# Third token tile of the second layer by products of half tiles, with weight buffers and weight steps moved

## The chip, the core and the metric

The kernel runs on one core of a Trainium2 chip. The core's engines work from queues of their own, each in the order in which its instructions were issued: TensorE (PE; its weight loads are listed apart as PEld), VectorE (DVE), ScalarE (ACT), GpSimd (POOL), and SyncE (SP), which issues most of the DMAs. The metric is the device time of one execution in microseconds (us), the median of the runs.

## The reference

```
# attention: b=2, h=8, s=768, d=64; blocks of 64, a decaying state per head
x = attention(q, k, v, lam)            # reshaped to 1536 tokens x 512
h = x @ w_in                           # 512 -> 2048
g = where(h >= 1, h, where(h <= -1, 0, (h + 1)**2 / 4))
x = g @ w_out                          # 2048 -> 512
y = (sigmoid(x @ w_gate) * (x @ w_val)) @ w_out2   # 512 -> 1536 -> 512
```

Tokens and results are float32, the weight matrices are float64. Every product of the two layers is made from high and low parts: high times high, low times high, high times low, three matmuls each.

## The kernel before

Attention runs first (lines 671 to 1001), in 16 units of 384 tokens. `u_load` fetches a unit's q, k, k and v rows as four slices; `scores` needs the first two. Attention's outputs are written as the high and low parts `xh` and `xl`. Beside it the first weight pieces are converted and the first layer begins.

A weight matrix is fetched in 68 pieces of 128 x 512 (`pieces`, line 73). Pieces 0 to 31 belong to the first layer; the second layer has 36, six for each group of two units: gate and value of both units, then both output slices. Group 18 has pieces 38 to 43, group 20 has 44 to 49, group 22 has 50 to 55, group 24 has 56 to 61, group 26 has 62 to 67. One step of the pipeline is a round (`w_steps`, line 175). In round k `w_float(k-1)` joins two limbs on VectorE (L122, L126), `w_high(k-2)` rounds to the high part on ScalarE (L130), `w_words(k)` takes the words of a raw tile apart on ScalarE (L108 into `r`, L115 and L116 into `c`), and `w_low(k-2)` makes the remainder on VectorE (L134). Buffers are rings: ten finished tiles (`NWP`), three raw tiles (`NRAW`), two `c` tiles and five `r` tiles. A round is put off while the finished tile whose buffer it needs is not in `used`.

Tokens are three tiles of 512. For tiles 0 and 1 together a pair of gate and value weights is multiplied by seven block products in place of eight (`pair`, line 430). It needs sums and differences of the weight blocks (`w_forms`, four half-width operations, L152) and their high and low parts (`w_forms_split`, line 155: ScalarE's copy L159, a subtraction L160). In the second layer's pairs both are on POOL (`prog["forms"] = pool`, line 625). Splits wait until `prog["room"]` allows them.

The order is written out by hand. In `second_layer` group 16 takes all three tiles one by one; from line 626 groups n0 = 18, 20, 22, 24, 26 follow with units n0 and n1 = n0 + 1: pair of n0, the projections of the group before for tile 2, pair of n1, projections of tiles 0 and 1, and between them tile 2 of each unit on its own (`single`, two calls of `hidden` with 12 matmuls each). A product is six matmuls: p0, p1, p0 (L449 copies it), p2, p0 (the fifth, after which L454 copies), p0, p2. A product that goes on accumulating in p0 waits until ScalarE has copied it. `pair_act` makes the high part, remainder, sigmoid and multiply of a result. `flush` adds four finished projections to `part` on VectorE (L306). Four PSUM banks serve the products, four the projections.

Of the kernel before, what the change touches and what calls it, by code (L numbers as in the profile page):

```python
# [7 lines left out]
F32 = mybir.dt.float32  # L8
F32R = mybir.dt.float32r
# [3 lines left out]
ALU = mybir.AluOpType  # L13
# [16 lines left out]
CST = 4 + PADW + P  # L30
NS = 2 * CU - 1
FORE, AFT = (6, 7), (5, 6)
JOBS = {4: ("W0", "", "", "F0", "", ""), 5: ("H0 W1", "", "F1", "", "H1 W2", ""),
# [5 lines left out]
WARM = 8  # L39
NWP, NRAW = 10, 3  # L40


@with_exitstack
def fused_kernel(ctx: ExitStack, tc: tile.TileContext, qkv, qd, cst, w1, w2, out):
# [42 lines left out]

    prog = {"loaded": 0, "round": 0, "room": True, "forms": dve, "split": False}
    used = set()

    attention_over = []

    def w_load():
        i = prog["loaded"]
        if i >= len(pieces) or i >= NRAW + max(0, prog["round"] - 1):
            return
        prog["loaded"] += 1
        n, o = pieces[i]
        raws[i] = rawp.tile([P, 512], I64, tag="raw", name=f"raw{i}")
        src = w1[n] if n < NF1 else w2[n - NF1]  # L100
        sp.dma_start(out=raws[i], in_=src[:, o:o + 512])

    def w_words(i):
        word = raws[i].bitcast(U32).rearrange("p (n two) -> p n two", two=2)
        lo, hi = word[:, :, 0], word[:, :, 1]
        r = tp.tile([P, 512], F32, tag="r", bufs=5, name=f"wr{i}")
        c = tp.tile([P, 512], I32, tag="c", name=f"wc{i}")
        act.activation(r, hi.bitcast(F32), AF.Copy, scale=2.0 ** -112)  # L108
        if not attention_over:
            act.activation(c, lo, AF.Copy, scale=2.0 ** -29)  # L110
            tmps[i] = r, c, hi
            return

        limb = lambda dt: c.bitcast(dt).rearrange("p (n two) -> p n two", two=2)
        act.activation(limb(U16)[:, :, 0], lo, AF.Copy, scale=2.0 ** -29)  # L115
        act.activation(limb(F16)[:, :, 1], hi.bitcast(F32), AF.Copy, scale=2.0 ** -60)  # L116
        tmps[i] = r, c, None
# [10 lines left out]
    def w_high(i):  # L128
        ws[i] = wp.tile([P, 2, 512], F32R, tag="w", name=f"w{i}")
        act.activation(ws[i][:, 0], tmps[i][0], AF.Copy)  # L130
# [24 lines left out]
    def w_forms_split(n):  # L155
        tiles = []
        for i, f in enumerate(forms[n]):
            t = fp.tile([P, 2, 512], F32R, tag="s", name=f"s{n}_{i}")
            act.activation(t[:, 0], f, AF.Copy)  # L159
            prog["forms"].tensor_tensor(out=t[:, 1], in0=f, in1=t[:, 0].bitcast(F32),  # L160
                                        op=ALU.subtract)
            tiles.append(t)
# [4 lines left out]
    def w_round():  # L167
        split = [n for n in forms if n not in ready and prog["split"]]
        if split and not prog["room"]:
            return  # L170
        w_steps()
        for n in split:
            w_forms_split(n)

    def w_steps():
        k = prog["round"]
        if k - 2 >= len(pieces):
            return
        if k - 2 >= NWP and k - 2 - NWP not in used:
            return  # L180
        prog["round"] += 1
        if 0 <= k - 1 < len(pieces):
            w_float(k - 1, dve)
        making = 0 <= k - 2 and k - 2 not in ws
        if making:
            w_high(k - 2)
        if k < len(pieces):
            while prog["loaded"] <= k:
                w_load()
            w_words(k)  # L190
        if making:
            w_low(k - 2, dve)
            w_forms(k - 2)
        w_load()
# [74 lines left out]
    def project(n, t, gs, first, last, now=True):  # L269
# [7 lines left out]
        for j in range(4):  # L277
            js = slice(j * P, (j + 1) * P)
            if two:
                ops = [(gh[:, js], w[:, 0]), (gh[:, js], w[:, 1]), (gl[:, js], w[:, 0])]  # L280
            else:
# [126 lines left out]
    def forms_second():  # L408
# [6 lines left out]
        return [x1, y2, x2, y1]  # L415

    def product(o, w, c, x, start):

# [11 lines left out]
    def pair(n):  # L430
# [29 lines left out]
        product(p2, s24, hw, x_at(1, 1), False)  # L460
        dve.tensor_tensor(out=r[1], in0=r[1], in1=p2, op=ALU.add)
        yield r

# [135 lines left out]
    def second_layer(waiting):  # L599
# [26 lines left out]
        for n0 in range(NF1 + GF, NF1 + NF2, GF):  # L626
# [8 lines left out]
            w_round()  # L635
            for _ in range(2 if n0 == NF1 + GF else 4):
                next(a)
            prog["room"] = False
            for p in waiting:
                w_round()  # L640
                project(*p, now=False)
            flush(p[0], p[1], (0, 1))
            ra, ga = next(a), {}
            flush(p[0], p[1], (2, 3))
            prog["room"] = True
            xa = pair_act(n0, ra, ga)
            for _ in range(5):
                next(b)
                next(xa)
            w_round()  # L650
            project(n0, 0, ga[0], True, False)
            w_round()
            rb, gb = next(b), {}
            ha = single(n0, 2, pair_act(n1, rb, gb))
            w_round()
# [15 lines left out]
    with ExitStack() as actx:  # L671
        kp = actx.enter_context(tc.tile_pool(name="kp", bufs=1))
        up = actx.enter_context(tc.tile_pool(name="up", bufs=UB))
# [10 lines left out]
        def u_load(i, js=range(2)):  # L684
# [10 lines left out]
            if i < NEARLY:  # L695

                t = [wp.tile([P, 2, 512], F32, tag="w", name=f"u{i}_{j}")
                     .rearrange("p a b -> p (a b)")[:, 0:2 * UT]
                     .rearrange("p (a t) -> p a t", a=2) for j in js]
                for j in js:  # L700
# [175 lines left out]
        def values(i):  # L876
# [11 lines left out]
            if i >= NEARLY:  # L888
                u_load(i + UB)

# [117 lines left out]
    for c in "hl":  # L1008
        xt[c] = late.tile([P, 3, HK, TT], F32R, name=f"xt{c}")
    attention_over.append(1)  # L1010
    with tc.manual_schedule():
        psx.close()
        for c in "ah":
            banks[c] = ctx.enter_context(
# [73 lines left out]
```

## Time and profile before

| | us |
|---|---|
| median of 3 runs (586.93 to 587.21) | 587.18 |
| the profiled execution's own time | 587.08 |
| its span, first to last instruction | 585.2 |
| TensorE busy | 579.0 |
| VectorE busy | 441.1 |
| ScalarE busy | 370.8 |

The span is the time between the first and the last instruction; 1.9 us of the execution lie around it. Busy time is the union of an engine's records. A matmul's record is longer than the step from one matmul to the next, so the starts tell the pace. In a timeline a row gives the start and the length in us, and behind it, in brackets, how long the engine had been idle and what ended that. Groups of the second layer begin at 344.56 (18), 390.80 (20), 437.04 (22), 483.28 (24) and 529.52 us (26).

### The profile page before, as it was taken

How to read it: one execution, taken by the hardware profiler on the slowest of the kernel's cores; microseconds unless marked ns; L12 is line 12 of the kernel's file. 1: busy time of each engine (PE TensorE's matmuls, PEld its weight loads, DVE VectorE, ACT ScalarE, POOL GpSimd, SP SyncE). 2: the span in 40 equal slices, each digit the busy share in tenths (PEclk: the TensorE clock that was granted, in tenths of full speed). 3: DMA queues.
4: the chain of work that ended last, by engine and by line, in shares of the span. 5: the costliest groups of instructions: out<-in, count | busy, mean ns of one | idle time of the engine just before them, and what ended most of it. 6: DMA issues, size and time to landing. Idle time of an engine off the chain costs nothing.

```text
span 585.2 us, 8061 instructions
## 1 busy us (share of the span) xinstructions
PE 579.0 (99%) x3074; PEld 481.4 (82%) x3074; DVE 441.1 (75%) x722; ACT 370.8 (63%) x653; POOL 71.3 (12%) x72
## 2 busy tenths in 40 slices
PE   8999999999999999999999999999999999999997
PEld 8987788888888888888888888888888888888885
DVE  5988798888897979797888996793693694684444
ACT  4678775996777777777874976772672773541220
POOL 3540000000000000000000002421412332150000
PEclk9999999999999999999999999999999999999999
DMA  8983340122112222221312223231231140000013
GB/s 336 401 317 109 108 144 1 37 92 80 46 72 73 72 73 72 73 72 38 107 38 72 84 96 109 72 109 36 73 108 37 38 120 22 1 0 2 0 73 143
DMA packets 15734, 52.00 MB, mean 89 GB/s; under 512 B 1744, under 2 KB 1872, under 8 KB 15696
## 3 DMA queue, kind: packets, MB, share of 16 engines
q1 hardware_dynamic: 15552, 51.39, 26.4%
q8 instruction: 24, 0.39, 0.3%
q10 hardware_dynamic: 144, 0.10, 0.1%
q14 instruction: 14, 0.11, 0.1%
HBM read 48.33 MB, written 3.15 MB: 88 GB/s over the span
## 4 chain that ended last, share of the span: by engine, by line
PE 93%; DMA 2%; DVE 2%; ACT 2%; issue 1%; SPq 0%; POOL 0%; DVEq 0%; POOLq 0%; ACTq 0%
PE a L284 38%; PE p L423 26%; PE h L229 8%; PE h L231 8%; PE h L230 8%; DMA u<-in_qkv 2%; PE s L821 2%; PE x L882 1%; PE x L901 1%; PE uu L839 1%; DVE part L306 0%; DVE r L265 0%; ACT r L256 0%; ACT r L261 0%; ACT gh L248 0%
## 5 line engine op out<-in xcount | busy, mean ns | idle before, releaser
L284 PE MATMUL a<-gh,w 128*128 128x512 f32 x384 | 118.6, 390 | 0.5 <-DVE w L134 0.5
L306 DVE TENSOR_TENSOR part<-part,a 128x512 f32<-128x512 f32 x132 | 83.3, 682 | 12.1 <-PE a L284 11.9
L284 PE MATMUL a<-w,gh 128*128 128x512 f32 x288 | 88.7, 389 | 0.0
L229 PE MATMUL h<-xh,w 128*128 128x512 f32 x224 | 87.6, 391 | 0.0
L230 PE MATMUL h<-xh,w 128*128 128x512 f32 x224 | 87.2, 389 | 0.0
L231 PE MATMUL h<-xl,w 128*128 128x512 f32 x224 | 87.1, 389 | 0.0
L284 PEld LDWEIGHTS a<-gh,w 128*128 128x128 f32 x384 | 72.0, 188 | 15.9 <-DVE w L134 0.9
L284 PE MATMUL a<-gl,w 128*128 128x512 f32 x192 | 74.7, 389 | 0.0
L284 PEld LDWEIGHTS a<-w,gh 128*128 128x128 f32 x288 | 54.1, 188 | 11.3
L284 PE MATMUL a<-w,gl 128*128 128x512 f32 x144 | 56.0, 389 | 0.0
L152 POOL TENSOR_TENSOR wr<-wr 128x256 f32<-128x256 f32 x16 | 13.1, 821 | 340.6 <-DVE w L134 340.0
L130 ACT ACTIVATE w<-wr 128x512 fp32r<-128x512 f32 x68 | 42.3, 622 | 17.7 <-DVE wr L126 17.5
L134 DVE TENSOR_TENSOR w<-wr,w 128x512 fp32r<-128x512 f32 x65 | 48.4, 745 | 4.0 <-ACT w L130 3.8
L126 DVE CUSTOM_DVE_ANT_0 wr<-wr,wc 128x1024 uint16<-128x1024 uint16 x68 | 48.1, 708 | 3.4 <-ACT wc L116 0.2
L229 PEld LDWEIGHTS h<-xh,w 128*128 128x128 f32 x224 | 42.1, 188 | 9.1 <-ACT r L261 0.2
L231 PEld LDWEIGHTS h<-xl,w 128*128 128x128 f32 x224 | 42.1, 188 | 8.8
L230 PEld LDWEIGHTS h<-xh,w 128*128 128x128 f32 x224 | 42.1, 188 | 8.6
L115 ACT ACTIVATE wc<-raw 128x512 uint16<-128x512 uint32 x61 | 47.9, 785 | 0.0
L108 ACT ACTIVATE wr<-raw 128x512 f32<-128x512 f32 x68 | 45.0, 662 | 4.2 <-POOL s L160 3.6
L116 ACT ACTIVATE wc<-raw 128x512 f16<-128x512 f32 x61 | 47.0, 771 | 0.0
L248 ACT ACTIVATE gh<-r 128x512 fp32r<-128x512 f32 x40 | 24.9, 624 | 31.7 <-DVE r L265 21.8
L284 PEld LDWEIGHTS a<-gl,w 128*128 128x128 f32 x192 | 36.0, 188 | 7.5
(121 smaller groups left out, 1028.7 us busy)
## 6 DMA issues: line engine op xcount, KB each, us to landing
raw<-in_w SPq DMA_DIRECT2D x68, 512.0 KB, 3.5
u<-in_qkv SPq DMA_DIRECT2D x22, 384.0 KB, 8.1
u<-in_qkv SPq DMA_DIRECT2D x4, 768.0 KB, 7.9
out<-part SPq DMA_DIRECT2D x12, 256.0 KB, 2.1
part<-in_qkv SPq DMA_DIRECT2D x2, 384.0 KB, 8.4
cs<-in_cst ACTq DMA_DIRECT2D x1, 98.0 KB, 3.8
```

The costliest lines, as they stand in the source:

```text
L108: act.activation(r, hi.bitcast(F32), AF.Copy, scale=2.0 ** -112)
L115: act.activation(limb(U16)[:, :, 0], lo, AF.Copy, scale=2.0 ** -29)
L116: act.activation(limb(F16)[:, :, 1], hi.bitcast(F32), AF.Copy, scale=2.0 ** -60)
L126: eng.tensor_tensor(out=ri, in0=ri, in1=c, op=ALU.add)
L130: act.activation(ws[i][:, 0], tmps[i][0], AF.Copy)
L134: eng.tensor_tensor(out=ws[i][:, 1], in0=r, in1=ws[i][:, 0].bitcast(F32), op=ALU.subtract)
L229: pe.matmul(h, lhsT=wh, rhs=xh[:, k, tt], start=(k == 0), stop=False)
L230: pe.matmul(h, lhsT=wl, rhs=xh[:, k, tt], start=False, stop=False)
L231: pe.matmul(h, lhsT=wh, rhs=xl[:, k, tt], start=False, stop=(k == NP - 1))
L284: pe.matmul(accs[j], lhsT=a, rhs=b_, start=(first and m == 0), stop=(last and m == 2))
L306: dve.tensor_tensor(out=o, in0=o, in1=accs[j], op=ALU.add)
L423: pe.matmul(o, lhsT=a, rhs=b_, start=(start and k == 0 and m == 0), stop=(k == HK - 1 and m == 2), skip_group_check=True)
```

## The change

In groups 20 to 26 tile 2 is no longer made by `single` but by `pair_third`: the seven block products on two halves of the tile, 256 tokens each, for both units side by side in one bank. That is 14 times six matmuls of 256 columns for 48 of 512. The sums and differences of the token blocks are made once, in group 20 (`forms_third`, 20 forming operations, 8 high parts and 8 remainders of 256 columns), spread over the steps of the two pairs by `along`. Room for them is made by closing a pool: finished weights keep nine tiles (`NWP`) and one of the pool `extra` (pieces 9, 19, 29, 39), raw tiles two and one of the pool up to piece 48, and `c` one and one of the pool up to piece 48. Forms are split at other places of a group, and from group 20 on the subtraction is VectorE's. In rounds 8 and 9 the high part and remainder of a piece come ahead of the float of the next (`LOW_FIRST`). Piece 8 is loaded once attention is over. Unit 13 of attention is loaded in two parts.

```diff
+LOW_FIRST = (8, 9)
...
-NWP, NRAW = 10, 3
+NWP, NRAW = 9, 2
+EXTRA_W, EXTRA_RAW = (9, 19, 29, 39), 48
...
         i = prog["loaded"]
-        if i >= len(pieces) or i >= NRAW + max(0, prog["round"] - 1):
+        more = 1 if i <= EXTRA_RAW else 0
+        if i >= len(pieces) or i >= NRAW + more + max(0, prog["round"] - 1):
+            return
+        if i == 8 and not attention_over:
             return
         prog["loaded"] += 1
         n, o = pieces[i]
-        raws[i] = rawp.tile([P, 512], I64, tag="raw", name=f"raw{i}")
+        pool_ = extra["pool"] if i % 3 == 2 and i <= EXTRA_RAW else rawp
+        raws[i] = pool_.tile([P, 512], I64, tag="raw", name=f"raw{i}")
...
-        c = tp.tile([P, 512], I32, tag="c", name=f"wc{i}")
+        pool_ = extra["pool"] if i % 2 and i <= EXTRA_RAW else tp
+        c = pool_.tile([P, 512], I32, tag="c", bufs=1, name=f"wc{i}")
...
     def w_high(i):
-        ws[i] = wp.tile([P, 2, 512], F32R, tag="w", name=f"w{i}")
+        if i not in EXTRA_W:
+            ring.append(i)
+        ws[i] = (extra["pool"] if i in EXTRA_W else wp).tile([P, 2, 512], F32R, tag="w", name=f"w{i}")
         act.activation(ws[i][:, 0], tmps[i][0], AF.Copy)
...
-            prog["forms"].tensor_tensor(out=t[:, 1], in0=f, in1=t[:, 0].bitcast(F32),
-                                        op=ALU.subtract)
+            eng = dve if prog["thirds"] else prog["forms"]
+            eng.tensor_tensor(out=t[:, 1], in0=f, in1=t[:, 0].bitcast(F32), op=ALU.subtract)
...
     def w_round():
         split = [n for n in forms if n not in ready and prog["split"]]
         if split and not prog["room"]:
-            return
+            if not prog["thirds"]:
+                return
+            split = []
+        if prog["thirds"]:
+            for n in split:
+                w_forms_split(n)
         w_steps()
         for n in split:
-            w_forms_split(n)
+            if n not in ready:
+                w_forms_split(n)
...
     def w_steps():
         k = prog["round"]
         if k - 2 >= len(pieces):
             return
-        if k - 2 >= NWP and k - 2 - NWP not in used:
+        i = k - 2
+        if i in EXTRA_W[1:]:
+            if EXTRA_W[EXTRA_W.index(i) - 1] not in used:
+                return
+        elif i not in EXTRA_W and i >= NWP and i not in ws and ring[-NWP] not in used:
             return
         prog["round"] += 1
+        making = 0 <= k - 2 and k - 2 not in ws
+        low = lambda: (w_low(k - 2, dve), w_forms(k - 2))
+        if making and k in LOW_FIRST:
+            w_high(k - 2)
+            low()
         if 0 <= k - 1 < len(pieces):
             w_float(k - 1, dve)
-        making = 0 <= k - 2 and k - 2 not in ws
-        if making:
+        if making and k not in LOW_FIRST:
             w_high(k - 2)
         if k < len(pieces):
             while prog["loaded"] <= k:
                 w_load()
             w_words(k)
-        if making:
-            w_low(k - 2, dve)
-            w_forms(k - 2)
+        if making and k not in LOW_FIRST:
+            low()
         w_load()
...
             if two:
-                ops = [(gh[:, js], w[:, 0]), (gh[:, js], w[:, 1]), (gl[:, js], w[:, 0])]
+                ah, al = (g[j] if isinstance(g, list) else g[:, js] for g in (gh, gl))
+                ops = [(ah, w[:, 0]), (ah, w[:, 1]), (al, w[:, 0])]
...
+    HT = TT // 2
+    xt2 = {}
+    third = lambda x, k, b: x[:, k * HK:(k + 1) * HK, 2 * TT + b * HT:2 * TT + (b + 1) * HT]
+    def forms_third():
+        last.close()
+        pool_ = ctx.enter_context(tc.tile_pool(name="third", bufs=1, reuse_waits="tile"))
+        for c in "hl":
+            xt2[c] = pool_.tile([P, 3, HK, HT], F32R, name=f"xt2{c}")
+        f = pool_.tile([P, HT], F32, name="f3")
...
+        def form(k, i, *terms):
...
+            def forming():
+                for m, (x, y, op) in enumerate(terms):
+                    a, b = (f if z is None else at(*z).bitcast(F32) for z in (x, y))
+                    dve.tensor_tensor(out=f, in0=a, in1=b, op=op)
+            def high_():
+                act.activation(hi_at, f, AF.Copy)
+            def rests():
+                dve.tensor_tensor(out=lo_at, in0=f, in1=hi_at.bitcast(F32), op=ALU.subtract)
+            return forming, high_, rests
...
+        add, sub = ALU.add, ALU.subtract
+        for k in range(HK):
+            made = [
+                form(k, 0, ((xh, 0, 1), (xh, 0, 0), sub), (None, (xl, 0, 0), sub),
+                     (None, (xl, 0, 1), add)),
+                form(k, 1, ((xh, 1, 1), None, sub), (None, (xl, 1, 1), add)),
+                form(k, 2, ((xh, 1, 0), None, sub), (None, (xl, 1, 0), add)),
+                form(k, 3, ((xh, 1, 1), (xh, 0, 1), sub), (None, (xl, 0, 1), sub),
+                     (None, (xl, 1, 1), add)),
+            ]
+            rests = None
+            for forming, high_, after in made:
+                steps_.append((lambda a=rests, b=forming: (a and a(), b()), high_))
+                rests = after
+            steps_.append((rests, lambda: None))
+        return steps_
...
+    def pair_third(n0):
...
+        ns = (n0, n0 + 1)
+        hw = HK * P
+        raw = lambda k, b: (third(xh, k, b), third(xl, k, b))
+        t_at = lambda i: (xt2["h"][:, i], xt2["l"][:, i])
+        p0, p1, p2 = (bank(f"t{n0}_{i}") for i in range(3))
+        r = [rest(f"v{n0}_{i}") for i in range(3)]
+        g, v = ([ws[index[n, o]] for n in ns] for o in (0, 512))
+        s31, s24 = ([ready[n][i] for n in ns] for i in range(2))
...
+        def both(o, w, c, x, start):
+            for i in range(2):
+                product(o[:, i * HT:(i + 1) * HT], w[i], c, x, start and i == 0)
+        both(p0, g, 0, raw(0, 0), True)
+        act.activation(r[0], p0, AF.Copy)
+        yield
+        both(p1, g, hw, raw(1, 0), True)
+        dve.tensor_tensor(out=r[0], in0=r[0], in1=p1, op=ALU.add)
+        yield
+        both(p0, s24, 0, t_at(1), False)
+        act.activation(r[1], p0, AF.Copy)
+        yield
+        both(p2, s31, hw, t_at(0), True)
+        yield
+        both(p0, s31, 0, raw(0, 1), False)
+        act.activation(r[2], p0, AF.Copy)
+        dve.tensor_tensor(out=r[2], in0=r[2], in1=p2, op=ALU.add)
+        act.activation(r[0], r[0], AF.Sigmoid)
+        yield
+        both(p0, v, hw, t_at(2), False)
+        dve.tensor_tensor(out=r[0], in0=r[0], in1=p0, op=ALU.mult)
+        both(p2, s24, hw, raw(1, 1), False)
+        dve.tensor_tensor(out=r[1], in0=r[1], in1=p2, op=ALU.add)
+        used.update(index[n, o] for n in ns for o in (0, 512))
         yield r
...
-            for _ in range(2 if n0 == NF1 + GF else 4):
-                next(a)
-            prog["room"] = False
+            thirds = n0 > NF1 + GF
+            if n0 == NF1 + 2 * GF:
+                made = forms_third()
+            def along(step):
+                begin, end = made.pop(0) if thirds and made else (None, None)
+                if begin:
+                    begin()
+                x = step()
+                if end:
+                    end()
+                return x
+            for _ in range(4 if thirds else 2):
+                along(lambda: next(a))
+            prog["room"], prog["thirds"] = thirds, thirds
             for p in waiting:
                 w_round()
                 project(*p, now=False)
+                prog["room"] = False
             flush(p[0], p[1], (0, 1))
             ra, ga = next(a), {}
             flush(p[0], p[1], (2, 3))
-            prog["room"] = True
+            prog["room"] = not thirds
...
             for _ in range(5):
-                next(b)
+                along(lambda: next(b))
                 next(xa)
             w_round()
             project(n0, 0, ga[0], True, False)
+            along(lambda: None)
...
             w_round()
...
-            ha = single(n0, 2, pair_act(n1, rb, gb))
+            xb = pair_act(n1, rb, gb)
+            if thirds:
+                c = pair_third(n0)
+                for _ in range(5):
+                    next(c)
+                    next(xb)
+                project(n1, 0, gb[0], False, True)
+                rc, gc = next(c), {}
+                xc = pair_act(n0, rc, gc)
+                next(xc)
+                prog["room"] = True
+                w_round()
+                prog["room"] = False
+                next(xc)
+                next(xc)
+                project(n0, 1, ga[1], True, False)
+                next(xc)
+                next(xc)
+                project(n1, 1, gb[1], False, True)
+                waiting = []
+                for i, n in enumerate((n0, n1)):
+                    at = lambda x: [gc[j // 2][x][:, i * HT + j % 2 * P:i * HT + j % 2 * P + P]
+                                    for j in range(4)]
+                    waiting.append((n, 2, (at(0), at(1)), n == n0, n == n1))
+                continue
+            ha = single(n0, 2, xb)
...
                 t = [wp.tile([P, 2, 512], F32, tag="w", name=f"u{i}_{j}")
                      .rearrange("p a b -> p (a b)")[:, 0:2 * UT]
-                     .rearrange("p (a t) -> p a t", a=2) for j in js]
+                     .rearrange("p (a t) -> p a t", a=2) if 2 * i + j < NWP else
+                     kp.tile([P, 2, UT], F32, name=f"u{i}_{j}") for j in js]
...
             if i >= NEARLY:
-                u_load(i + UB)
+                for js in ((0,), (1,)) if i + UB == NHALVES + 1 else ((0, 1),):
+                    u_load(i + UB, js)
...
+    last = ctx.enter_context(ExitStack())
+    extra["pool"] = last.enter_context(tc.tile_pool(name="extra", bufs=1, reuse_waits="tile"))
     attention_over.append(1)
     with tc.manual_schedule():
         psx.close()
+        w_load()
```

## Rows read from the trace of the kernel before

**Rows 1.** Busy us (share of the span) and instructions of each engine, whole span.

```profile
PE 579.0 (99%) x3074; PEld 481.4 (82%) x3074; DVE 441.1 (75%) x722; ACT 370.8 (63%) x653; POOL 71.3 (12%) x72
```

**Rows 2.** Busy us (and instructions) of each engine by stretch, groups 20 and 22.

```profile
core 0: us, PE busy (x) PEld busy (x) DVE busy (x) ACT busy (x) POOL busy (x), PEclk, DMA share, GB/s
...
390.80:437.00 46.20, 46.20 (x205) 38.30 (x204) 31.13 (x49) 26.27 (x46) 12.64 (x12) 1.00 0.23 69
437.00:483.30 46.30, 46.30 (x206) 38.32 (x206) 31.23 (x49) 26.29 (x46) 12.63 (x12) 1.00 0.23 69
```

**Rows 3.** Timeline, TensorE and its loads, 500 to 503: start, us, engine, line.

```profile
500.05 0.39 PE L423 MATMUL p<-xl,w 128*128 128x512 f32 x1
500.05 0.41 PEld L423 LDWEIGHTS p<-xh,w 128*128 128x128 f32 x2
...
502.77 0.39 PE L423 MATMUL p<-xtl,s 128*128 128x512 f32 x1
```

**Rows 4.** Groups by line and shape, weight loads: xcount, busy us, mean ns, idle before.

```profile
L423 PEld LDWEIGHTS p<-xh,w 128*128 128x128 f32 x128 | 24.0, 188 | 5.0
...
L882 PEld LDWEIGHTS x<-pT,u 128*64 128x64 f32 x180 | 9.6, 137 | 1.2 <-issue 0.7
```

**Rows 5.** Timeline, weight loads in attention, 24 to 29.

```profile
23.97 1.42 PEld L821 LDWEIGHTS s<-u 64*128 64x128 f32 x24 [0.17 <-issue]
...
27.44 0.72 PEld L839 LDWEIGHTS uu<-u,kd 128*64 128x64 f32 x20
```

**Rows 6.** Timelines, VectorE and TensorE, 70 to 74.

```profile
70.85 0.42 DVE L122 TENSOR_SCALAR wr<-wr 128x512 uint32<-128x512 uint32 x1
...
71.91 0.68 DVE L134 TENSOR_TENSOR w<-wr,w 128x512 fp32r<-128x512 f32 x1
...
71.75 0.39 PE L284 MATMUL a<-gh,w 128*128 128x512 f32 x1
72.65 0.50 PE L284 MATMUL a<-gh,w 128*128 128x512 f32 x1 [0.51 <-DVE w L134]
```

**Rows 7.** Timeline, TensorE, 34 to 36.

```profile
34.94 0.94 PE L821 MATMUL s<-u 64*128 64x128 f32 x12 [0.21 <-DMA u<-in_qkv]
```

**Rows 8.** Groups by line, the subtraction of a form's split on either engine.

```profile
L160 DVE TENSOR_TENSOR s<-wr,s 128x512 fp32r<-128x512 f32 x16 | 10.3, 685 | 0.0
...
L160 POOL TENSOR_TENSOR s<-wr,s 128x512 fp32r<-128x512 f32 x16 | 24.9, 1575 | 81.1 <-ACT s L159 81.1
```

**Rows 9.** Timelines, VectorE and POOL, 460 to 470, one row of each.

```profile
464.12 1.39 DVE L134 TENSOR_TENSOR w<-wr,w 128x512 fp32r<-128x512 f32 x1 [0.31 <-ACT w L130]
...
463.13 3.54 POOL L160 TENSOR_TENSOR s<-wr,s 128x512 fp32r<-128x512 f32 x2 [19.36 <-ACT s L159]
```

**Rows 10.** Timeline, VectorE, 328.9 to 331.4: two dependent operations of 256 columns.

```profile
329.66 0.89 DVE L152 TENSOR_TENSOR wr<-wr,wr 128x256 f32<-128x256 f32 x2
```

**Rows 11.** Groups by line and shape, ScalarE's copy of 256 columns.

```profile
L860 ACT ACTIVATE ld<-qp 128x256 f32<-128x256 f32 x7 | 2.8, 404 | 0.0
```

**Rows 12.** Timeline, VectorE, 436 to 441: the turn from group 20 to 22.

```profile
435.57 2.48 DVE L306 TENSOR_TENSOR part<-part,a 128x512 f32<-128x512 f32 x4
437.96 0.42 DVE L122 TENSOR_SCALAR wr<-wr 128x512 uint32<-128x512 uint32 x1
438.41 0.69 DVE L126 CUSTOM_DVE_ANT_0 wr<-wr,wc 128x1024 uint16<-128x1024 uint16 x1
439.75 0.69 DVE L134 TENSOR_TENSOR w<-wr,w 128x512 fp32r<-128x512 f32 x1 [0.64 <-ACT w L130]
```

**Rows 13.** Timeline, ScalarE, 437 to 445: the same turn.

```profile
438.60 0.60 ACT L443 ACTIVATE q<-p 128x512 f32<-128x512 f32 x1 [3.67 <-PE p L423]
...
440.17 0.80 ACT L115 ACTIVATE wc<-raw 128x512 uint16<-128x512 uint32 x1
440.82 0.78 ACT L116 ACTIVATE wc<-raw 128x512 f16<-128x512 f32 x1
441.44 0.59 ACT L449 ACTIVATE q<-p 128x512 f32<-128x512 f32 x1
```

More of the change, by code (lines that the diff above doesn't have):

```diff
@@ L84, in fused_kernel @@
     whole, forms, ready = {}, {}, {}
-    prog = {"loaded": 0, "round": 0, "room": True, "forms": dve, "split": False}
+    prog = {"loaded": 0, "round": 0, "room": True, "forms": dve, "split": False, "thirds": False}
     used = set()
     attention_over = []
+    extra = {}
+    ring = []
     def w_load():
         i = prog["loaded"]
-        if i >= len(pieces) or i >= NRAW + max(0, prog["round"] - 1):
+        more = 1 if i <= EXTRA_RAW else 0
+        if i >= len(pieces) or i >= NRAW + more + max(0, prog["round"] - 1):
+            return
+        if i == 8 and not attention_over:
             return
@@ L415, in forms_second @@
         return [x1, y2, x2, y1]
+    HT = TT // 2
[7 more added lines that the diff above has]
+        f = pool_.tile([P, HT], F32, name="f3")
+        steps_ = []
+        def form(k, i, *terms):
+            at = lambda x, j, b: third(x, j, b)[:, k]
+            hi_at, lo_at = ((at(xh, 0, 1), at(xl, 0, 1)) if i == 3 else
+                            (xt2["h"][:, i, k], xt2["l"][:, i, k]))
+            def forming():
[23 more added lines that the diff above has]
+        return steps_
     def product(o, w, c, x, start):
@@ L461, in pair @@
         dve.tensor_tensor(out=r[1], in0=r[1], in1=p2, op=ALU.add)
+        yield r
+    def pair_third(n0):
[31 more added lines that the diff above has]
+        used.update(index[n, o] for n in ns for o in (0, 512))
         yield r
@@ L651, in second_layer @@
             project(n0, 0, ga[0], True, False)
+            along(lambda: None)
+            assert not thirds or not made
             w_round()
             rb, gb = next(b), {}
-            ha = single(n0, 2, pair_act(n1, rb, gb))
+            xb = pair_act(n1, rb, gb)
[24 more added lines that the diff above has]
+            ha = single(n0, 2, xb)
             w_round()
@@ L671, in fused_kernel @@
     with ExitStack() as actx:
-        kp = actx.enter_context(tc.tile_pool(name="kp", bufs=1))
+        kp = extra["pool"] = actx.enter_context(tc.tile_pool(name="kp", bufs=1))
         up = actx.enter_context(tc.tile_pool(name="up", bufs=UB))
```

## Prediction

> **What bounds the kernel now.** I read the engine totals first: TensorE is busy 99% of the span, VectorE 75% [rows 1]. The totals average stages, so next the table by stretch: groups 20 and 22 of the second layer take 46.2 and 46.3 us, TensorE fills both, VectorE is busy 31 us in each [rows 2]. A busy TensorE need not be at its peak, so I look at starts: between 500.05 and 502.77 twelve matmuls of 512 columns begin, one per 226.7 ns [rows 3], and 204 of them (84 for two pairs, 48 for the singles, 72 projections) make 46.24 us, the whole group. Nothing waits: the group costs what its matmuls cost. Every term below is therefore matmul time saved, or a new wait of TensorE.
>
> **The third tile by block products.** In groups 20, 22, 24 and 26 the two units' singles (48 matmuls of 512 columns) give way to seven products of 6 matmuls for each of two units, 84 of 256 columns. Removed: 48 x 226.7 = 10.88 us a group. Added: 84 times a price that no row shows, since nothing here streams 256 columns. From below: at exactly half, 113.3 ns. In attention two row groups renew a 128-column weight load every (1.42-0.19)/11 = 112 ns [rows 5], so loads of that size can follow each other that fast. From above: the record of such a load is 188 ns, 50 ns more than one of 64 columns [rows 4], and 188 would be the price if a matmul had to wait for the whole record. For a value: in attention a pair of 128-column matmuls takes 112 ns and one of 64 columns (0.72-0.14)/9.5 = 61 ns [rows 5], so 51 ns are per 64 columns and some 10 ns are fixed. With 10 fixed, 256 columns cost (226.7-10)/2 + 10 = 118 ns. I take that, as the row with the same engine and element size, with 113 to 124 as its near ends. Then a group saves 10.88 - 84 x 0.118 = 0.95 us, four save **3.8 us** (1.9 to 5.4). Break-even is 10.88/84 = 129.5 ns.
>
> The Trainium skill (TensorE: Matmul & The Clock Gate, Back-to-back issue gap) gives N/2.4 + 2.5 ns warm: 109 ns at 256, which would save 1.7 us a group. The same rule gives 215.8 ns at 512, where the rows have 226.7, so the trace disagrees and I keep 118.
>
> **Two remainders first, unit 13 in parts.** TensorE stops once behind the weight pipeline: a matmul starts at 72.65 where 71.98 was due, behind the remainder (L134) that VectorE begins at 71.91, after two operations of the next piece from 70.85 [rows 6]. Put first, it begins at 70.85 and ends before the matmul is due: 0.67 us back, and the slower first starts after the stop, together **0.8 us**. It cannot cost more than the two operations it passes, 1.1 us, which work a round ahead. Unit 13: TensorE waits 0.21 us for its load [rows 7], starts included some **0.3 us** (0 to 0.4), back if queries and keys land first.
>
> **Moves that I cost at nothing.** The extra pool keeps ten weight tiles, three raw tiles and two c tiles until piece 39 or 48, each buffer reused at the old distance. Piece 8's load moves behind the end of attention on SP's queue, some 58 us, and all later loads queue behind it; ScalarE reads it at 70.57 in the trace and a load takes 3.5 us in the median, so 8 us cover it. Without that cover it would cost what it is late. Finished weights stand a group ahead of their use before; by the new ring piece 49 waits for 40, and then 53 is made at the end of group 20, needed 15 us into group 22. Cover remains.
>
> **What VectorE and ScalarE get.** A third tile by blocks needs seven operations of each for four before: +3 each. Subtractions of four forms move from POOL (1,575 ns) to VectorE (685 ns) [rows 8], +2.7 us a group. POOL's use does slow VectorE: a remainder takes 1.39 us beside one [rows 9]. In group 20 come 28 operations of 256 columns, 0.45 us each [rows 10], 12.6 us, and 8 ScalarE copies of 0.40 [rows 11], all within its first 27 us, beside three rounds of 1.7 and 17 operations of 0.60 us, 15.3 us, of VectorE's other work there. And from piece 49 on there is one c tile: ScalarE's words of a piece wait for VectorE's float of the piece before, issued in the same round. Queued behind on ScalarE are the evacuations that TensorE waits for.
>
> **Stall in group 20.** Times from the group's start. Starting as group 22 does now, VectorE ends the flushes at 0.9, float at 2.1 and the remainder at 3.4 [rows 12]; three forming operations then end at 4.7, the high part on ScalarE at 5.1, and the copy of p0, due 4.4, is done at 5.6: the fifth product, due 5.44, waits 0.2. Each form costs its operations and 0.45 for the trip to ScalarE. Carried on this way, the second pair's copy of p0 ends 0.35 late for its sixth product, and its multiply, behind float and remainder, frees a bank 0.7 late for the third tile's second product. Together **1.3 us** (0.5 to 2.5).
>
> **Stall at the start of groups 22 and 24.** After the third tile's last product (ends 40.0) VectorE queues one addition (40.2), two form subtractions, float and remainder to 43.7, and the remainder of the first half to 44.3. ScalarE's words may begin their second part only after float, at 43.2; they take 1.27, and the sigmoid behind them ends at 45.1. Then multiply (45.9), high part (46.55), remainder (47.2), the four flushes (0.60 apart) to 49.6, and the next float to 50.75. The group turned at 45.4, so this float ends 5.3 into the next one, where before it ended at 2.1 [rows 12]. There ScalarE's words wait for it (5.4), and behind their 1.27 the copy of p0 begins at 6.7, where before it began at 4.40 [rows 13], the group having begun at 437.04. It ends at 7.3; the fifth product was due at 5.44: 1.9 us. Beside POOL's forming, which starts at 43.8, multiply and remainder take up to 0.5 longer [rows 9]: 2.1 us each, **4.2 us** (2.5 to 5.5). Group 26 has no words left in that round: nothing. Add 0.2 for the bank of the third tile in 22 and 24. Before, two c tiles and a light tail (flushes over at 0.9) cover all this.
>
> **Sum**, from the profiled execution's own 587.08 us (span 585.2 plus 1.9 around it; the median of the runs is 587.18, 0.1 above): -3.8 -0.8 -0.3 +1.3 +4.2 +0.2 = +0.8, so **587.9 us**. The saving is real and is given back at three starts of groups. Its own range: most saving and least stall 587.1 - 5.4 - 1.2 + 3.0 = 583.5; least saving and most stall 587.1 - 1.9 - 0.8 + 8.2 = 592.6; I call it 585.0 to 591.0.
>
> **Rivals.**
> 1. *The tail is in time.* If VectorE and ScalarE run the chain faster than I add it up, or enough of it lies beside the last projections (10.9 us from the third tile's end to the fifth product, against my chain of 12.7), the starts of 22 and 24 cost nothing. Then 587.1 - 4.9 + 0 to 1.5 = 582.2 to 583.7, say 583. For it: TensorE has not one gap in these groups now, and VectorE is still idle a third of each group [rows 2]. Against it: the chain is serial, and the idle third lies elsewhere.
> 2. *Halves at 112 ns*, the pace at which attention renews its loads [rows 5], the stalls as worked: 84 x 0.112 = 9.41, four times 1.47 saved, 587.1 - 5.9 - 1.1 + 5.7 = 585.8. By the skill's 109 ns it would be 584.9.
> 3. *The weight load sets the pace* (slower). In the trace each load begins with the matmul before it and is recorded at 188 ns, hidden under 226.7 [rows 3, 4]. If the next matmul needs all of it, a half costs 188: 84 x 0.188 = 15.8, +4.9 a group, 587.1 + 19.6 - 1.1 + about 1 = 607. It decides from 129.5 ns on. Against it: 112 ns between loads [rows 5], there with two row groups in turn.
> 4. *Load and stream one after the other.* 100 for the load (128 columns at 50 ns per 64 [rows 4]) and 113 for the stream are 213 ns a half: 17.9 for 10.9, +7.0 a group, 587.1 + 28.0 - 1.1 = 614. Against it: 226.7 ns for 512 columns leaves no 100 for a load, unless a column takes far less than the 0.42 ns that I count. The Trainium skill (TensorE: Matmul & The Clock Gate, Packing small matmuls) says weight loads overlap running matmuls only where the row group differs; it would mean this rival, and the 226.7 of whole-array matmuls speaks against it here.
>
> **How the numbers follow.** Forecast 0.57, rival 1 0.27, rival 2 0.08, rival 3 0.05, rival 4 0.03. Some 0.2% (1.2 us) is what a measurement can tell from no change: faster is below 586.0, slower above 588.4. Of the forecast's 0.57, 0.13 lie below, 0.22 between, 0.22 above. Faster: 0.27 + 0.08 + 0.13 = 0.48, shaded to 0.46 as rival 2 reaches into the middle; same 0.23; slower 0.31. Cases of both signs share the chance, so the range runs from rival 1 without any stall (582.0) to the top of the forecast (591.0), leaving out rivals 3 and 4 and about a tenth beyond the ends.
>
> **What the profile would show.** Right: starts 118 ns apart in the new products; no gap near 72; one TensorE gap of about 2 us at the fifth product of groups 22 and 24, ended by ScalarE's copy of p0, whose words waited for VectorE's float; three small gaps in group 20; none in group 26. Groups of about 46.6 (20), 47.4 (22, 24) and 45.3 us (26). Wrong: starts above 130 ns, groups of 45.3 without gaps, or the waits on another engine than ScalarE.

## The result, and the profile after

| | before | after |
|---|---|---|
| median, us | 586.99 (6 runs) | 591.47 (6 runs) |
| ratio, 95% interval | | 1.0071 (1.0058 to 1.0084) |
| the profiled execution, us | 587.08 | 591.48 |
| its span, us | 585.2 | 589.6 |

The change made the kernel slower by 0.7%. Forecast was 587.9 us in a range of 582.0 to 591.0; the time lies above it. First the table by stretch: busy us (and instructions) of TensorE, its loads, VectorE, ScalarE and POOL. The rows are groups 20, 22 and 24, and as many us from the start of group 26 on as a group took before; the last columns are the granted clock of TensorE, the DMA share and GB/s.

```profile
core 0: us, PE busy (x) PEld busy (x) DVE busy (x) ACT busy (x) POOL busy (x), PEclk, DMA share, GB/s
390.10:436.20 46.10, 46.05 (x241) 39.08 (x240) 37.79 (x73) 25.08 (x46) 4.50 (x6) 1.00 0.14 43
436.20:484.70 48.50, 45.84 (x242) 39.32 (x241) 34.43 (x56) 28.56 (x49) 7.58 (x9) 1.00 0.22 66
484.70:534.70 50.00, 47.34 (x241) 40.37 (x240) 34.41 (x56) 28.61 (x49) 7.45 (x9) 0.97 0.18 53
534.70:580.90 46.20, 46.20 (x245) 39.92 (x244) 28.89 (x45) 14.77 (x26) 2.14 (x3) 1.00 0.09 32
```

Beside [rows 2]: group 20 takes as long as before, group 22 takes 2.2 us more and group 24 3.8 us more. TensorE is idle for 2.7 us in each of groups 22 and 24, and in group 24 its granted clock is 0.97 as well. VectorE is still idle for 14 and 16 us there. Group 26 has no gap. The timeline of TensorE shows where the idle time stands (start, us, engine, line; in brackets the idle time and what ended it), first in group 22, then in group 24.

```profile
441.44 0.39 PE L497 MATMUL p<-xtl,s 128*128 128x512 f32 x1
444.49 0.73 PE L497 MATMUL p<-xh,s 128*128 128x512 f32 x2 [2.66 <-ACT q L523]
...
489.87 0.39 PE L497 MATMUL p<-xtl,s 128*128 128x512 f32 x1
492.92 0.73 PE L497 MATMUL p<-xh,s 128*128 128x512 f32 x2 [2.66 <-ACT q L523]
...
494.36 0.63 PE L497 MATMUL p<-xl,s 128*128 128x512 f32 x1
494.79 1.05 PE L309 MATMUL a<-w,gh 128*128 128x512 f32 x2
```

Both gaps are the forecast's: the fifth product of the first pair, waiting for ScalarE's copy of p0 (L523, L449 before). From start to start they are 3.05 us where 0.23 are due, 2.82 us lost. After the second, from 494.0 on, the matmuls start 0.43 us apart instead of 0.227 for some 3.4 us. Granted clock around both, same columns with TensorE alone:

```profile
441.40:444.50 3.10, 0.44 (x3) 1.00 0.00 0
444.50:448.00 3.50, 3.50 (x15) 1.00 0.50 150
489.80:493.00 3.20, 0.54 (x4) 1.00 0.00 0
493.00:494.00 1.00, 1.00 (x5) 0.98 0.51 123
494.00:497.40 3.40, 3.40 (x10) 0.51 0.34 123
497.40:500.00 2.60, 2.60 (x13) 1.00 0.00 0
```

The clock went to its lower level of 1.2 GHz after the second gap, 1.0 us behind its end, and not after the first. That cost 1.6 us, the difference of groups 24 and 22. Five of the six executions took 591.3 to 591.9 us at a mean granted clock of 0.996 or 0.997; the sixth took 589.55 at 0.999, by its clock without the fall.

Next, VectorE and ScalarE around the turn from group 20 to 22 (at 436.22), the view of [rows 12, 13].

```profile
430.96 0.69 DVE L572 TENSOR_TENSOR v<-v,t 128x512 f32<-128x512 f32 x1 [0.64 <-PE t L497]
431.56 1.29 DVE L172 TENSOR_TENSOR s<-wr,s 128x512 fp32r<-128x512 f32 x2
...
433.22 0.69 DVE L135 CUSTOM_DVE_ANT_0 wr<-wr,wc 128x1024 uint16<-128x1024 uint16 x1
...
435.88 1.20 DVE L688 TENSOR_TENSOR v<-v,v 128x512 f32<-128x512 f32 x1 [0.76 <-ACT v L686]
437.84 1.21 DVE L681 TENSOR_TENSOR gl<-v,gh 128x512 fp32r<-128x512 f32 x1 [0.76 <-ACT gh L690]
438.97 2.47 DVE L331 TENSOR_TENSOR part<-part,a 128x512 f32<-128x512 f32 x4
441.36 0.41 DVE L131 TENSOR_SCALAR wr<-wr 128x512 uint32<-128x512 uint32 x1
441.81 0.69 DVE L135 CUSTOM_DVE_ANT_0 wr<-wr,wc 128x1024 uint16<-128x1024 uint16 x1
...
433.95 0.79 ACT L124 ACTIVATE wc<-raw 128x512 uint16<-128x512 uint32 x1 [0.83 <-DVE wr L135]
...
437.18 0.63 ACT L690 ACTIVATE gh<-v 128x512 fp32r<-128x512 f32 x1 [1.33 <-DVE v L688]
...
442.60 0.78 ACT L124 ACTIVATE wc<-raw 128x512 uint16<-128x512 uint32 x1 [3.13 <-DVE wr L135]
443.24 0.75 ACT L125 ACTIVATE wc<-raw 128x512 f16<-128x512 f32 x1
443.86 0.57 ACT L523 ACTIVATE q<-p 128x512 f32<-128x512 f32 x1
```

Every link of the chain is there in the forecast's order. Before, the flushes were over 0.9 us into the group; now they begin 2.75 us into it (438.97), the float follows at 5.1, and ScalarE, idle for 3.13 us, may only then go on with its words; the copy stands behind them. POOL's four forming operations run from 434.59 to 438.50, beside the multiply (L688) and the remainder (L681) at 437.84, which take 1.20 and 1.21 us where such operations take 0.69 alone. Last, the start of the third tile's products, the view of [rows 3].

```profile
417.94 0.40 PE L497 MATMUL t<-xh,w 128*128 128x256 f32 x2
418.18 0.28 PE L497 MATMUL t<-xl,w 128*128 128x256 f32 x1
418.30 0.40 PE L497 MATMUL t<-xh,w 128*128 128x256 f32 x2
...
419.02 0.40 PE L497 MATMUL t<-xh,w 128*128 128x256 f32 x2
```

From 417.94 to 419.02 nine start: 120 ns each. That is the step in all four groups.

### The profile page after: what moved, and what is told of

Read it like the earlier page. It is cut to its first block, busy times and chain, and to the rows that moved or that the text cites. A ratio compares the mean times of both kernels' runs of the same rounds, so it can differ in the third digit from the quotient of the medians.

```text
span 589.6 us, 8401 instructions
## 1 busy us (share of the span) xinstructions
PE 579.1 (98%) x3218; PEld 486.6 (83%) x3218; DVE 460.5 (78%) x774; ACT 382.0 (65%) x673; POOL 55.1 (9%) x60
## 4 chain that ended last, share of the span: by engine, by line
PE 83%; DVE 10%; ACT 4%; issue 1%; DMA 1%; SPq 0%; POOL 0%; ACTq 0%; DVEq 0%; POOLq 0%
PE a L309 34%; PE p L497 23%; PE t L497 7%; PE h L254 5%; PE h L253 5%; PE h L255 5%; DVE part L331 2%; DVE wr L135 2%; PE s L975 1%; PE x L1036 1%; PE x L1056 1%; ACT wc L124 1%; DVE wr L131 1%; DVE pT L1004 1%; DVE wr L133 1%
## 5 line engine op out<-in xcount | busy, mean ns | idle before, releaser
L253 PE MATMUL h<-xh,w 128*128 128x512 f32 x160 | 62.7, 392 | 0.0
L254 PE MATMUL h<-xh,w 128*128 128x512 f32 x160 | 62.3, 389 | 0.0
L255 PE MATMUL h<-xl,w 128*128 128x512 f32 x160 | 62.2, 389 | 0.0
L145 DVE TENSOR_TENSOR w<-wr,w 128x512 fp32r<-128x512 f32 x65 | 46.3, 713 | 1.9 <-ACT w L141 1.7
L497 PE MATMUL p<-xh,s 128*128 128x512 f32 x128 | 40.1, 394 | 5.4 <-ACT q L523 5.3
L497 PE MATMUL p<-xh,w 128*128 128x512 f32 x128 | 39.4, 389 | 0.0
L497 PE MATMUL p<-xth,s 128*128 128x512 f32 x128 | 39.4, 389 | 0.0
L253 PEld LDWEIGHTS h<-xh,w 128*128 128x128 f32 x160 | 30.0, 188 | 6.7 <-issue 0.2
```

Of the source, the lines that this page charges most:

```text
L145: eng.tensor_tensor(out=ws[i][:, 1], in0=r, in1=ws[i][:, 0].bitcast(F32), op=ALU.subtract)
L253: pe.matmul(h, lhsT=wh, rhs=xh[:, k, tt], start=(k == 0), stop=False)
L254: pe.matmul(h, lhsT=wl, rhs=xh[:, k, tt], start=False, stop=False)
L255: pe.matmul(h, lhsT=wh, rhs=xl[:, k, tt], start=False, stop=(k == NP - 1))
L497: pe.matmul(o, lhsT=a, rhs=b_, start=(start and k == 0 and m == 0), stop=(k == HK - 1 and m == 2), skip_group_check=True)
```

## The experiments

Theory 1 is the forecast's chain: ScalarE's words wait for VectorE's float, which stands behind late flushes, and TensorE's copy stands behind the words. Its main rival says that VectorE simply has too much to do. The kernel before took 586.91 to 587.04 us on the chips of these runs, so 0.1 us between two of them says nothing.

**Words behind the copy.** In groups 22 to 26 the round is issued after the third product's copy.

```diff
-            w_round()
+            if n0 <= NF1 + 2 * GF:
+                w_round()
...
-            for _ in range(4 if thirds else 2):
+            for s in range(4 if thirds else 2):
                 along(lambda: next(a))
+                if s == 1 and n0 > NF1 + 2 * GF:
+                    w_round()
```

> The changed kernel with one round moved: in groups 22, 24 and 26 it is issued after the copy of p0 that the fifth product waits for, not ahead of it. Theory 1 (ScalarE's words wait for VectorE's float behind the late flushes, and the copy stands behind them): both gaps of 2.82 us at the fifth product of groups 22 and 24 vanish, and with them the 1.6 us of halved clock that follow the second, so 591.5 - 5.6 - 1.6 = 584.3 us; groups 22 and 24 take 45.4 to 45.8 us. Theory 2 (VectorE has too much to do in these groups, whatever the order): the wait turns up at another product within the same group, groups stay at 47 us or more, 589 us or more.

Measured 583.82 us, ratio to before 0.9945 (0.9929 to 0.9962). Groups 22 and 24 by stretch:

```profile
436.20:481.70 45.50, 45.50 (x242) 39.35 (x240) 34.28 (x56) 28.60 (x49) 7.53 (x9) 1.00 0.23 70
481.70:527.20 45.50, 45.50 (x242) 39.37 (x241) 34.27 (x56) 28.64 (x49) 7.52 (x9) 1.00 0.18 59
```

and its ScalarE in the same stretch:

```profile
440.50 0.60 ACT L523 ACTIVATE q<-p 128x512 f32<-128x512 f32 x1 [2.12 <-PE p L497]
...
443.19 0.80 ACT L124 ACTIVATE wc<-raw 128x512 uint16<-128x512 uint32 x1 [1.00 <-DVE wr L135]
```

VectorE is as busy as in the changed kernel (34.3 us a group) and TensorE has no gap: the copy runs at 440.50, when its product is done, and the words still wait for the float, with nobody behind them. The order on ScalarE's queue is the cause; VectorE's load is not.

**One gap alone.** The same move in group 22 only (condition `n0 == NF1 + 3 * GF`).

> The changed kernel with the round moved behind the copy in group 22 alone, so that only the start of group 24 keeps its gap of 2.82 us. Theory 1 for the time: 591.5 - 2.8 = 588.7 if the clock still falls after the gap of group 24, 587.0 if it does not. For the clock: if any idle stretch of 2.8 us can bring it down, it falls as often as before after this one; if it takes the second of two, it no longer falls.

588.09 us, ten executions between 586.74 and 589.62. Six had granted clocks of 0.994 to 0.997 and took 588.0 us or more, four had 0.999 or 1.000 and took 587.1 or less. One gap is enough for the clock to fall, and it does not fall each time; without the fall the time is theory 1's 587.0. With it the executions took 1.0 to 1.7 us more, the one at 0.994 2.6. In the trace the clock had fallen before the gap ended (489.95); same columns with TensorE alone:

```profile
489.90:493.00 3.10, 3.05 (x7) 0.52 0.52 174
```

**Forming later on POOL.** The four operations of the tail's round are issued after the last remainder.

```diff
-        low = lambda: (w_low(k - 2, dve), w_forms(k - 2))
+        held = prog.get("hold")
+        low = lambda: (w_low(k - 2, dve), held.append(k - 2) if held is not None else w_forms(k - 2))
...
+                prog["hold"] = []
                 w_round()
...
+                for i in prog.pop("hold"):
+                    w_forms(i)
```

> The changed kernel with POOL's four forming operations of the round at the end of a group issued after the third tile's last remainder, so that POOL no longer runs beside VectorE's multiply and remainder (1.20 and 1.21 us there). Theory 1: the chain is serial, so both operations at 0.7 us shorten each gap by 1.0 us, 2.82 to about 1.8; 591.5 - 2.0 = 589.5 with the clock still falling, 587.9 if the shorter gap no longer lets it fall. Theory 2 (VectorE's load): the same work on VectorE less 1.0 of its 37 us, so the gaps shrink by a third at most of that. Theory 3 (raw loads or finished weights late): no change.

591.99 us (589.65 to 593.02 in four executions), the gaps unchanged at 3.05 us from start to start. POOL shows why the edit did nothing:

```profile
434.54 1.12 POOL L163 TENSOR_TENSOR wr<-wr 128x256 f32<-128x256 f32 x1 [28.32 <-DVE w L145]
```

Its queue is empty and it waits only for the finished piece, so it starts at the same moment as before. The time is what theory 3 expected, but since the edit moved nothing, the run decides between no theories.

**Forming on VectorE in the next group.** Now they are made on VectorE, behind the addition of the second product there.

```diff
+                if s == 1 and n0 > NF1 + 2 * GF:
+                    prog["forms"] = dve
+                    for i in held:
+                        w_forms(i)
+                    prog["forms"] = pool
```

> The changed kernel with the four forming operations of the round at the end of a group made on VectorE in the next group, behind the first addition there, so that nothing of POOL runs beside the tail's multiply and remainder. (Issued later on POOL alone they had started at the same moment, since nothing stands before them in that queue.) Theory 1: multiply and remainder fall from 1.20 to 0.7 us, the gaps at the starts of groups 22 and 24 from 2.82 to about 1.8 us: 591.5 - 2.0 = 589.5 if the clock still falls once, 587.7 if it does not. Theory 2 (VectorE's load): 1.8 us more for VectorE in each group, so no gain or a loss.

587.74 us, all ten executions between 587.52 and 587.86. VectorE in the tail, and the gap:

```profile
435.88 0.69 DVE L689 TENSOR_TENSOR v<-v,v 128x512 f32<-128x512 f32 x1 [0.75 <-ACT v L687]
437.33 0.69 DVE L682 TENSOR_TENSOR gl<-v,gh 128x512 fp32r<-128x512 f32 x1 [0.76 <-ACT gh L691]
...
443.46 0.73 PE L498 MATMUL p<-xh,s 128*128 128x512 f32 x2 [1.63 <-ACT q L524]
```

Both operations fall to 0.69 us, and the gaps to 2.02 us from start to start, 1.79 us lost, although VectorE does 1.8 us more in each group. The neighbour on POOL is worth the other 1.03 us of each gap of 2.82. With these gaps the clock did not fall in ten executions.

**Form subtractions back on POOL**, in the tail's round only.

```diff
-            eng = dve if prog["thirds"] else prog["forms"]
+            eng = dve if prog["thirds"] and not prog.get("tail") else prog["forms"]
```

> The changed kernel with the two form subtractions of the round at the end of a group back on POOL (1.58 us each there, 0.69 on VectorE). Theory 1 (a serial chain through ScalarE's words, which need the buffers that these subtractions free): words begin their first part about 1.7 us later, and the gaps at the starts of groups 22 and 24 grow from 2.82 to about 4 us each, 591.5 + 2.4 = 593.9. Theory 2 (VectorE's load): VectorE has 1.2 us less in the tail of each group, so the gaps shrink to about 1.6 and the time falls to 589 or less.

592.14 us in the median of four, 589.93 where the clock did not fall, gaps of 3.08 us from start to start: 0.03 more than in the changed kernel, which neither theory had. VectorE and POOL tell why:

```profile
432.12 1.67 DVE L135 CUSTOM_DVE_ANT_0 wr<-wr,wc 128x1024 uint16<-128x1024 uint16 x1
433.71 1.78 DVE L145 TENSOR_TENSOR w<-wr,w 128x512 fp32r<-128x512 f32 x1
...
431.68 3.27 POOL L172 TENSOR_TENSOR s<-wr,s 128x512 fp32r<-128x512 f32 x2 [25.29 <-ACT s L170]
```

The two operations leave VectorE, and float and remainder beside them take 1.67 and 1.78 us instead of 0.69. Removing work from VectorE bought nothing because of where it went. In this trace the clock fell behind the first gap (TensorE alone, granted clock 0.79) and not behind the second:

```profile
441.40:448.00 6.60, 3.91 (x12) 0.79 0.25 79
```

**A single c tile in the kernel before.** From piece 49 on, nothing else changed.

```diff
-        c = tp.tile([P, 512], I32, tag="c", name=f"wc{i}")
+        c = tp.tile([P, 512], I32, tag="d" if i % 2 and i <= 48 else "c", bufs=1, name=f"wc{i}")
```

> The kernel before with a single c tile from piece 49 on and nothing else changed. Theory 1 (the gap needs both the single tile and VectorE's late tail): VectorE ends its flushes 0.9 us into a group there and the float at 2.1, so the words' second part, at 3.1, never waits: 587.0 us, no gap. Theory 2 (the single tile alone makes the wait): gaps at the starts of groups 22 and 24, 588 us or more.

596.37 us, ratio 1.0160 (1.0143 to 1.0176): theory 1 is wrong here. TensorE waits for the copy of p0 at the starts of groups 20, 22 and 24 (us in total, times, longest), and VectorE and ScalarE at the turn to group 22 (439.23 here) show that in this kernel the late tail comes from the single tile itself.

```profile
PE p L423 <- ACT q L449: 6.9, 3, 2.5
...
437.38 0.69 DVE L593 TENSOR_TENSOR r<-r,h 128x512 f32<-128x512 f32 x1 [1.38 <-ACT r L592]
...
441.15 0.69 DVE L249 TENSOR_TENSOR gl<-r,gh 128x512 fp32r<-128x512 f32 x1 [1.43 <-ACT gh L248]
441.76 2.48 DVE L306 TENSOR_TENSOR part<-part,a 128x512 f32<-128x512 f32 x4
...
439.22 0.80 ACT L115 ACTIVATE wc<-raw 128x512 uint16<-128x512 uint32 x1 [0.80 <-DVE wr L126]
...
445.39 0.78 ACT L115 ACTIVATE wc<-raw 128x512 uint16<-128x512 uint32 x1 [2.71 <-DVE wr L126]
...
446.67 0.56 ACT L449 ACTIVATE q<-p 128x512 f32<-128x512 f32 x1
```

Each round lets ScalarE wait for VectorE's float and then VectorE for ScalarE's next result (1.38, 1.43 us idle), so the flushes slide from 1.5 us ahead of the turn [rows 12] to 2.5 us behind it, with no third tile by blocks in sight. Here three rounds stand in the tail of a group. The changed kernel's group 18, which still makes the third tile unit by unit, has the same single tile and two rounds there, and it is not late: its flushes begin 0.8 us ahead of the turn at 390.11, and the fifth product of group 20 waits 0.2 us.

```profile
389.32 2.48 DVE L331 TENSOR_TENSOR part<-part,a 128x512 f32<-128x512 f32 x4
```

So the single tile makes the tail late by itself in the kernel before; in the changed kernel, whose later groups have one round in the tail, the third tile by blocks has a part in it, as the forecast had it. That is read from one trace: the changed kernel with two c tiles was not run, so no run shows what the single tile is worth there.

**The low remainders behind**, in the kernel with the words behind the copy (`LOW_FIRST = ()`).

> The kernel with the words behind the copy (583.8 us) without the two remainders moved ahead. Theory 1: the stop near 72 us returns with 0.8 us, but the stop of 0.4 us near 81 us, which the earlier TensorE ran into, goes: about +0.3, 584.1 us. Theory 2, the forecast's term: the whole 0.8 us comes back, 584.6 us.

584.20 us, +0.38. The stop is back with 0.71 us of idle, and the small one near 81 us is gone:

```profile
72.23 0.50 PE L309 MATMUL a<-gh,w 128*128 128x512 f32 x1 [0.71 <-DVE w L145]
```

**Unit 13 in one piece**, in the same kernel.

> The kernel with the words behind the copy (583.8 us) with unit 13 loaded in one piece. Theory 1 (the wait for queries and keys near 34 us): it returns and costs 0.4 to 0.5 us, 584.3 us. Theory 2 (piece 8's load moved out of attention made the room): no change, 583.8 us.

584.25 us, +0.43, and the wait of [rows 7] is back:

```profile
34.77 0.94 PE L978 MATMUL s<-u 64*128 64x128 f32 x12 [0.21 <-DMA u<-in_qkv]
```

The parts are what removed it. The traces give less than the medians: from the first matmul of these scores (33.59 to 33.77 us) to the start of group 20 they have 356.34 us with both edits, 356.58 with unit 13 whole and 356.79 with the remainders behind, so 0.24 for the unit and 0.45 for the remainders.

**Quarters.** The same products streamed in 128 columns.

```diff
-            for i in range(2):
-                product(o[:, i * HT:(i + 1) * HT], w[i], c, x, start and i == 0)
+            for i in range(4):
+                qs = slice(i % 2 * P, (i % 2 + 1) * P)
+                product(o[:, i * P:(i + 1) * P], w[i // 2], c, [z[:, :, qs] for z in x],
+                        start and i == 0)
```

> The kernel with the words behind the copy (583.8 us) with the third tile's products streamed in quarters, 168 matmuls of 128 columns a group for 84 of 256, the same result. Theory 1 (a fixed 13.3 ns beside 0.417 ns a column, as 226.7 ns at 512 and 120 ns at 256 columns have it): starts 66.7 ns apart, 11.2 us a group for 10.1, 583.8 + 4.5 = 588.3 us. Theory 2 (weight loads of 128 columns follow each other no faster than in attention): starts 107 to 112 ns apart, 18 to 18.8 us a group, 616 to 619 us.

618.94 us, theory 2. A weight load and a matmul now start every 112 ns: 418.13 to 420.81 holds 24 steps.

```profile
418.13 0.19 PEld L497 LDWEIGHTS t<-xl,w 128*128 128x128 f32 x1
418.24 0.30 PEld L497 LDWEIGHTS t<-xh,w 128*128 128x128 f32 x2
...
420.81 0.19 PEld L497 LDWEIGHTS t<-xl,w 128*128 128x128 f32 x1
```

That is the 112 ns at which loads of 128 columns follow each other in [rows 5], and not the 66.7 ns that the stream alone would take by theory 1. So at 128 columns the load sets the pace; no run changed the load without the stream. The Trainium skill (TensorE: Matmul & The Clock Gate, LDWEIGHTS (loading the stationary operand)) gives 128/1.2 = 107 ns for such a load; the trace has 5 ns more.

**The best version.** The round behind the copy in group 20 as well (`n0 > NF1 + GF`).

> The kernel with the words behind the copy (583.8 us) with the same move in group 20 as well. There TensorE waits 0.3 us at the fifth product, 0.2 near 415 us and 0.1 to 0.2 in small steps. Theory 1 (the copy of p0 stands behind words and the first high part): the first wait goes, 583.5 us, or the later ones grow by what VectorE's round now takes between the forms, 583.8 to 584.2. Theory 2 (the order doesn't matter there): no change.

583.39 us, ratio to before 0.9939 (0.9924 to 0.9954), the fastest of all. The gap at the fifth product of group 20 is gone, the one near 415 us stays at 0.2 us.

## Why the prediction was wrong, point by point

Two steps failed. The sum had no term for TensorE's clock, which fell and cost 1.6 us. And it put POOL's neighbourhood in the starts of groups 22 and 24 at 0.2 us each, where the runs give 1.03. The mechanism of those starts was right. The one execution without the fall took 589.55 us, inside the range. The sum's own upper end was 592.6, which holds the measured time; I put the end of the range at 591.0 without a reason.

- **The saving.** 84 matmuls at 120 ns make 10.08 us for 10.88: 0.80 us a group for the forecast's 0.95, 3.2 for 3.8 in four. (84 times 0.118 is 9.91, so the forecast's own price gave 0.97.) The miss is small: the 10 ns of fixed time came from the pace of weight loads in attention; at 512 and 256 columns the two prices give 0.417 ns a column and 13.3 fixed. That 118 came so near was luck in part: it is another operation's pace, and the 61 ns behind it divide by 9.5 where ten pairs of loads have nine steps (64 ns, and 121 for a half). Rivals 3 and 4 (188 and 213 ns) fall, and rival 2's 112 ns was not reached at 256 columns; it is what 128 columns take.
- **Remainders and unit 13.** Forecast 0.8 and 0.3, found together 0.69 (group 20 starts at 390.11 for 390.80). By the traces above the remainders give 0.45 and the unit 0.24. The stop went, but TensorE ran into VectorE's copy of an accumulator near 81 us, 0.4 us, which is not there when the stop is. I had not asked what is late next.
- **Group 20.** Forecast 1.3 of stall, found 0.7: the multiply that I had late for the third tile's second product was in time.
- **The starts of groups 22 and 24.** Mechanism, place and engine as forecast; the mis-sized term is POOL's neighbourhood. The forecast had 1.9 us for the chain and 0.2 for POOL; without POOL the runs gave 1.79, with it 2.82. Each of the two operations beside POOL takes 0.5 us longer, 1.03 us together, and I had put 0.2 in the sum and 0.5 as the most, although [rows 9] held a doubling. Rival 1 falls; the 10.9 us of cover were too few.
- **The clock.** The sum had no term for what an idle TensorE does to its own clock: 1.6 us in the profiled execution. This term was missing, not mis-sized, and it carries the time out of the range.
- **Two c tiles and a light tail.** The forecast named them as two covers of the starts before. In the kernel before they are not two: with a single c tile its tail is late as well.

Together, against the forecast's +0.8: starts of groups 22 and 24 with the bank's 0.2 +1.6 (6.0 for 4.4), clock +1.6, halves +0.6, early terms +0.4, group 20 -0.6, make the 3.6 us by which the profiled execution was slower than forecast.

## What to carry to other kernels

A ring with one buffer turns a step of one engine into a wait for another; look up what is queued behind that step, and issue the copy that the bounding engine needs ahead of it. Moving work off a loaded engine helps only if the new neighbour does not slow it, and issuing work later on an empty queue does not make it run later. Price an idle gap of the bounding engine with what it may do to its clock.

## What the runs showed of the hardware

- Gaps of 2.8 us let TensorE's granted clock fall to its lower level of 1.2 GHz in most executions: by their mean clock five of six in the changed kernel, three of four in each of the two runs that kept its gaps, six of ten with one gap; three gaps of 2.2 to 2.6 us in the kernel before with one c tile did so in four of four. Gaps of 1.79 us did not in ten executions with two each. In the traces the low stretch lasted 3.4 us; it began between 0.5 us before and 1.0 us after the end of a gap, and cost 1.6 us in the changed kernel.
- With whole-array weights of 128 columns a matmul starts every 226.7 ns at 512 columns, 120 ns at 256 and 112 ns at 128. The rule beside rival 4, of the Trainium skill (TensorE: Matmul & The Clock Gate, Packing small matmuls), that weight loads overlap running matmuls only across row groups, does not hold in these traces: 120 ns leave no room for a load (112 ns) and a stream (256 columns at 0.417 ns, 107 ns) one after the other.
- VectorE's operations of 512 columns on two operands outside PSUM took 1.2 to 1.8 us in most cases beside POOL's (1.20 and 1.21 in the changed kernel, 1.39 in [rows 9], 1.67 and 1.78 with the subtractions on POOL), where they take 0.69 alone. Additions with one operand in PSUM stayed at 0.68 beside POOL (`q<-q,p` at 465.43 us in the kernel before, with POOL busy until 466.67).
